# Clustered attention and a Hyena layer on one core: the written order of the steps drawn anew from group 6's scores on

## The chip, the cores and the metric

The kernel runs on one core of one Trainium2 chip. The time is the device time of one execution in microseconds (us); less is better. A core has the engines PE (matrix products), DVE, ACT and POOL (element work of several kinds), SP (which issues transfers) and 16 DMA engines. Each engine works through a queue of its own in order and waits at an instruction until what it needs is there.

## The reference, cut

```python
q, k, v: (4, 8, 768, 64); centroids: (8, 16, 64)
q_assign = argmax(einsum('bhsd,hcd->bhsc', q_n, c_n))      # q, k, centroids normed
k_assign = argmax(einsum('bhsd,hcd->bhsc', k_n, c_n))
scores = 1/sqrt(64) * q @ k.T, where(q_assign == k_assign), else -1e9
attn = softmax(scores);  x = (attn @ v) laid out as (4, 768, 512)

proj = x @ w_proj;  x1, x2, x3 = proj split in three      # w_proj (512, 1536)
x2_conv = irfft(rfft(x2) * rfft(filter))                  # along the 768 positions
out = (x1 * x2_conv * x3) @ w_out                         # (4, 768, 512)
```

## The kernel before, in words

**Tiling.** The 32 heads are worked in 8 groups of four heads (group 6 is the second last), each group in two halves of two heads. Two groups make one of the four batches, and behind every second group stands the Hyena layer of that batch.

**A half of a group** (`attention`): for each of six key tiles three score products into one PSUM bank each (L643, in 64-column halves by `product`, L71), three exps on ACT (L657, L660) into a `p` tile, one product with v (L671, "pv"), and on DVE the sum of the `p` tiles (L688 for the first two, L692 "acc" for the others). The row sums in `acc` are then folded by POOL's accumulating DMAs (L725), go through DRAM by SP (L729 dd, L731 dp), are summed on DVE (L735), inverted (L737), and come back spread over the partitions (L738 dr, L742 rb). L772 multiplies with them and writes `xT`, the input of the Hyena layer.

**The routing of the next group** (`routing`): loads of q and k (L286) into four `qkraw` buffers, a transpose on DVE, called the swap here (L560), copies to the `aug` tiles, products with the centroids (L589, "sim"), transposes (L594), the maximum (L602), the one-hot (L603), its transpose (L606), a prefix product on PE (L610, of the transposed one-hot), its two forms on ACT (L612, L617), and mask transfers of them into `aug` by SP (L491). The v loads are L301.

**The Hyena layer** (`hyena`): U products (L809) and their sums and differences, products with the DFT table and with the filter's spectrum (L833, whose results L837 adds), G products (L71 on behalf of L875) with the gate on DVE (L886) or a copy on ACT, the inverse transform I, the folds (L922), the product y2 (L929 in two parts for the last, L934), the output products W (L945 for earlier batches, L951 for the last, there in a first part of three quarters and a last quarter), copies out of PSUM (L957) and outputs (L966, in the last batch's end L962, from SP or ACT). In the last batch, negated tables (L846 and the two copies at L850 and L852) are written into load buffer `qkraw[0]`, so they need the swap that reads it last to be over.

**What sets the order.** No scheduler runs: the string `ORDER` (L126 to L229) lists all 1,976 steps of the program, each as a letter of an engine and the number of the step, and for a step that takes PSUM banks the banks behind a colon. `P1053:3` is step 1053 on PE into bank 3. Each engine's queue is this list cut down to its letter, and a step waits for the steps that it depends on and for the last reader of its bank. Steps that read or write SBUF heavily on DVE and POOL are marked as locked: a locked POOL step waits for the last locked DVE steps ahead of it in the list; a DVE step doesn't wait for a POOL step.

Of the kernel before, what the change touches and what calls it, by code (L numbers as in the profile page):

```python
# [126 lines left out]
A30 S43 P0:7 G12 A42 P1:6 S44 G23 P2:7 V16 A34 A48 P3:6 S41 G22 A46 P4:7 P5:6 S47 G17 G14 G11 P6:7 V49 P7:6 G19 S45  # L127
V31 P8:7 G29 V50 P9:6 P10:7 V32 V33 V51 A35 A36 V52 V15 P72:6 V37 G24 P70:7 A53 G18 A54 S126 V73 P38:5 A71 S125 V55
P66:4 V39 G20 P64:3 A67 V56 S124 A65 P78:4 V57 S123 A69 V58 P76:3 A62 V75 A60 V79 A59 G61 P101:7 G74 V77 A63 P99:6 G27
V80 P95:4 S130 P93:2 G13 V96 A102 S127 V21 A100 V81 P144:4 P151:3 A94 S128 P252:7 V82 G68 P254:6 S129 A253 P146:2 G25  # L130
V145 A255 S122 V40 P88:7 P83:1 V152 A89 G103 P107:6 V147 S290 V84 A90 A153 V85 A98 P248:2 V104 P246:5 V92 G97 P185:3
V87 S286 A247 P192:4 S137 P105:0 G134 A186 V86 V91 A249 S287 P210:5 A193 V106 P258:3 P260:2 V108 G199 A259 P264:4 A261
V109 P266:3 A265 P196:7 G28 S301 P187:2 V110 A267 P194:4 G139 S295 A188 P220:0 V257 P270:63 S296 A221 V111 G26 A195
A211 G200 S136 P204:0 V272 P202:4 A197 P140:5 V271 P212:2 A203 P189:1 P222:7 S289 G250 V273 A213 S132 A190 P112:2
P148:6 A141 V115 P218:3 G201 P117:1 A223 P206:4 S133 V119 P214:5 A205 P230:7 V116 S298 A207 G138 P228:0 V150 V274 S300
A215 A263 S293 P191:45 V209 A269 S131 P198 A120 A113 V149 S291 G256 V275 A118 S292 A114 P208 G135 A121 V217 A229 S299
A219 P302:2 P321:1 A231 P309:0 S297 P276:6 V225 P226:3 A310 P216 A303 S294 A277 P304:2 A227 S288 V316 P279:0 P319:7
A322 P224 V233 A305 A268 P306:2 P232 A307 V159 A278 V157 A281 P313:2 V155 A234 P235:6 V160 A280 P311:1 P308:45 A314
V158 S283 A236 V433 G262 S245 A312 P327:6 S282 A251 P339:2 V439 G318 P323:0 P337:1 S237 P315 A328 V436 S463 A320 G317
S284 A324 V430 P347:6 S468 P335:3 A338 P329:7 S464 P331:0 V326 A340 P325 S285 A336 S465 A330 P373:3 A332 P343:2 S460  # L140
V162 P371:1 P345:7 A374 S472 P333 V334 A344 S459 A346 S458 P378:2 A434 P369:7 V163 P388:3 S461 P341 A348 V342 S362
A372 S238 A379 P376:1 S462 A370 P442:06 V384 S469 A377 V350 A432 S473 P390:1 P349 A389 S467 A391 V444 A431 G435 P398:3
V443 P476:1 P394:7 A351 G161 V445 P352:2 A395 P380:6 A399 P406:0 G154 V446 P404:7 P375:45 A353 A381 S354 V447 A405
P386:6 G383 A407 V239 P396:2 V716 P474:7 S240 P402:3 A387 P410:0 P382 A397 V719 G385 S746 A403 S355 A411 P412:3 G363
V156 P451:2 A477 P448:6 S745 P414:0 G368 P392 V164 A475 S242 A449 V393 S241 A450 P400 S470 A438 A453 V401 P481:6 A452
P485:7 A413 P166:1 S454 P408 A415 S466 A486 V356 V409 S455 A167 P165:0 S357 A482 P483:7 P495:3 P416 A171 S456 V417
A484 A496 P491:6 P478:7 A169 P499:2 V172 P419:3 G437 A479 V170 A500 G441 P174:7 A420 V168 P493:1 A418 G364 P511:2 S421
P509:3 V488 P173:0 G365 A492 P480:45 V243 A494 V244 A510 S422 V175 P507:1 A177 G489 P487 S359 V722 A508 S471 A512 G490
S749 V178 P655:1 P517:2 A656 P501:3 S358 V176 P503:7 A502 P519:6 P653:1 V498 P497 A504 A718 P660:7 A721 P515:3 P505
A440 V423 V506 S424 A516 S457 P513 A518 S534 A520 S429 V514 A654 P674:2 P662:3 S748 P657:6 A675 P670:0 S747 P680:1  # L150
A663 P521 S751 V725 A658 A681 V522 P728:36 A523 A671 A661 V360 P524:1 V361 P142:7 A525 P664:0 V730 S425 G668 P180:2
A665 V729 P672:1 S526 A143 P659:45 V731 A181 S426 A673 V669 P762:7 P682:1 V732 P179:0 A683 S527 P690:6 P678:3 A183
P666 V733 G667 S757 A679 V184 A691 P686:3 G367 A763 V182 P694:2 G366 P696:6 P688:1 A695 V528 P760:0 V427 S529 P764:7
A697 P676 V677 A765 A717 P684 A689 V428 A687 V685 P698:1 A761 P769:3 P734:7 A720 P692 A699 V693 A770 P771:1 P700 A735
S530 A736 S531 A772 V701 P737:7 P781:3 S744 A702 P767:0 P779:1 P785:6 S752 A738 P797:2 P766:45 A768 S750 A782 G703
S759 A786 P795:0 S756 A798 V532 A780 V533 A739 S758 V774 A724 P535:3 V886 G775 P537:2 V536 S914 P793:1 G776 P777:7
S740 V538 P789:3 P540:6 A778 V539 A726 S755 P787:7 V784 P542:2 A788 S753 A541 P545:7 S741 A790 G704 V543 P803:6 S754
P547:3 A546 V792 A804 P773 S915 A723 A794 V548 S743 P805:6 A727 V544 P801:1 G551 S742 P582:7 V549 A796 S822 P783 A806
V889 G553 A888 V895 S919 P791 A887 G705 S715 V800 A583 S917 P825:6 A890 P840:0 P842:3 P799 A802 V892 A826 A841 P823:1
V808 A843 P898:27 A824 V550 P852:3 P832:1 G810 P848:0 A853 S706 V900 P844:6 S929 P807 A833 V899 G552 S923 A849 V901  # L160
P554:0 A809 S918 V902 P557:7 P830:2 A845 P834:1 P827:3 V555 A831 S916 P578:6 G838 V556 A828 P934:2 A579 V558 P829:45
S926 A835 G837 V559 S885 V903 P850:1 S707 P858:7 P860:6 S920 P864:0 A859 V839 P930:3 P836 A851 V561 G811 A861 S927
V847 A865 S921 P856:6 P562:1 A931 P866:0 A935 P565:7 V560 P963:3 A857 P868:2 P846 V855 A867 A893 P941:0 A869 P854 V564
A942 V863 A891 P932:0 P904:2 G812 P593:6 A933 A905 P907:0 V567 P862 A594 A906 V871 A909 P951:2 A908 P949:6 P870 A952
V563 A950 G569 V708 P570:2 A872 V566 S813 P937:1 G873 S924 P573:6 V709 A938 V568 S911 P965:0 P955:7 A966 V572 P939:1
S910 P936:45 A964 V1174 A956 G946 S814 A940 V1177 P957:3 P947:7 P973:0 P959:1 A948 S710 V571 P943 G944 A958 V575 A896
S928 V574 G945 P953 S1205 S925 G874 V954 A974 S922 A960 P1115:0 S712 P967:6 P975:1 A968 P1122:3 P1113:2 V576 P971:7
A976 P584:6 S1207 V962 A1123 P580:1 S913 A1114 P1132:3 A972 S711 P1118:2 P961 A1116 V577 S912 G875 A1119 V970 P1111:2
P586:70 A1112 P969 A587 V581 A894 V978 P1120:1 A897 P977 A1133 V589 P1130:2 G980 V588 P599:3 S876 A1131 V1180 P597:7
G590 A1121 V815 P1144:2 S1211 A598 P601:01 G591 V585 S1213 A1145 V1183 P1136:7 P595:6 A602 G592 A1137 V600 P1148:2  # L170
A1179 V816 P1186:73 V603 S817 A1149 V604 S877 A1175 V596 S1212 P1146:2 V713 P612:6 A1147 V606 P1220:1 V714 S1209 A613
P1140:0 P608:2 V1187 A979 G981 P1156:6 V1188 A1141 P1117:45 V1189 G1125 S819 A609 P1128:2 V1127 S1203 P1138:0 P1152:7
A1129 P1154:3 V1190 P1124 S818 A1139 A1157 S1206 V1126 A1153 S992 P1218:6 V605 P616:20 G982 A1221 V1135 A1219 P1222:7
P1229:1 P1134 A1155 A617 V878 A1223 G607 P1227:3 V1191 A1181 P1142 A1230 V879 V619 S880 A1228 P1192:1 V618 P1195:7
P1225:6 A1193 V1143 P1235:3 P614:2 A1184 S983 P1253:0 S1208 A1194 P1150 A1196 V820 A1197 V1151 A1226 P1158 S1198 A1236
S984 P627:6 V821 P610:3 V1234 S881 A1160 V621 P1237:7 S882 A628 P629:1 V615 A1185 V1159 P1239:2 P1263:6 A1238 P1224:45
A1240 V630 G620 P1247:2 P1251:1 A1248 P623:7 V985 G1161 A1252 V611 A624 V986 P631:32 V622 S987 A1264 S1199 P1245:1
A632 P1231 V883 A1246 V884 A1178 V633 P1255:6 G1232 P1243:1 V634 P625:7 A1244 V1347 P1259:3 A1254 G1233 P1261:2 P1241
S989 V626 A1348 S988 G1162 V1242 A1260 S1216 P1249 A1262 S1210 A1256 S1204 A1182 P1306:3 P1257 V1250 A1176 S1202 P1265
V990 S1200 V991 P1302:6 S1214 P1281:2 A1267 V1258 G1163 P1310:7 P993:0 S1215 A1282 P995:1 A994 S1217 V1266 A1311  # L180
P1003:2 S1378 A1303 P1290:7 P1005:6 A1004 V636 A1291 G1268 V996 P1308:2 P998:0 A1309 V1006 G635 A1307 V997 P1285:7
S1164 P1000:2 S1201 V1344 G637 A999 P1298:1 A1286 P1036:3 V1001 S1173 A1299 P1040:0 V1007 A1037 G1008 P1316:1 S1280
V1002 P1283:7 P1055:6 A1317 V1350 A1284 G1009 P1314:2 P1292:1 A1041 P1051:3 S1165 V1353 A1315 P1288:0 G1269 A1056
# [1052 lines left out]
```

## Time and profile before

| | |
|---|---|
| three timed runs, us | 351.40, 352.58, 352.62 (median 352.58) |
| the profiled execution's own time, us | 351.8 |
| its span, us | 350.0 |
| granted TensorE clock, mean | 0.997 |
| page's longest groups: pv products (L671), busy us on PE | 141.3 |
| exps L660 and L657, busy us on ACT | 108.8 and 56.3 |
| acc L692, busy us on DVE | 111.9 |
| DMA moved, MB | 45.68 |

Span and rows are those of one profiled execution; 1.8 us of its time lie outside the span. A row of the timeline gives the start, the length, the engine, the source line, the operation with its output and input, and how many instructions were put together; in brackets stands the idle time of the engine ahead of it and what ended that. In the page's groups, the busy time and the mean length of one stand behind the bar.

The end of the span is the output of the last batch: W products up to 344.5, copies, and transfers that move until 348.4.

### The profile page before, as it was taken

The numbers are of one execution on the slowest core, as the hardware profiler recorded it, in microseconds if no ns is written. First come the engines' busy times: TensorE is split into PE (matmuls) and PEld (weight loads), VectorE is DVE, ScalarE is ACT, GpSimd is POOL, SyncE is SP. The second block draws the span as 40 slices with busy tenths as digits, with TensorE's granted clock in tenths as the row PEclk, the third lists the DMA queues.
The fourth block names the chain that finished last, engine by engine and source line by source line (L and its number), as shares of the span: only waits on it lengthen the run. The fifth ranks groups of instructions, "written<-read, shape, count | busy, mean of one in ns | idle before, by whom it ended". The sixth has DMA issues, their size and how long they took to land.

```text
span 350.0 us, 8306 instructions
## 1 busy us (share of the span) xinstructions
PE 338.0 (97%) x3140; PEld 225.5 (64%) x3143; DVE 327.5 (94%) x453; ACT 274.4 (78%) x514; POOL 148.6 (42%) x175
## 2 busy tenths in 40 slices
PE   7899999999999999999999999999999999999993
PEld 3544455465756687866657687756677666678872
DVE  7999999999989999999999999989988999989992
ACT  5899999998989798889888798798896674433442
POOL 7486308232234517262337735461425034067610
PEclk9999999999999999999999999999999999999998
DMA  9989693997698997897697979655586411230044
GB/s 168 206 181 209 116 170 49 155 165 173 105 167 146 160 148 105 146 151 123 117 168 154 149 80 222 87 99 123 112 211 109 93 11 65 91 122 0 19 165 180
DMA packets 126323, 45.68 MB, mean 131 GB/s; under 512 B 113720, under 2 KB 118604, under 8 KB 126284
## 3 DMA queue, kind: packets, MB, share of 16 engines
q1 hardware_dynamic: 120396, 34.25, 50.4%
q0 software_dynamic: 2960, 9.77, 18.3%
q10 hardware_dynamic: 2928, 1.15, 1.4%
q8 instruction: 24, 0.39, 0.5%
q14 instruction: 15, 0.12, 0.2%
HBM read 31.59 MB, written 7.40 MB: 111 GB/s over the span
## 4 chain that ended last, share of the span: by engine, by line
PE 66%; ACT 15%; DMA 6%; DVE 4%; issue 4%; POOL 3%; SPq 1%; ACTq 0%; DVEq 0%; POOLq 0%
PE bank L71 32%; PE pair L671 24%; ACT p L660 6%; PE bank L809 5%; DMA qkraw<-in_q_dram 3%; ACT p L657 2%; ACT aug L249 2%; DMA dr<-dn 2%; PE bank L589 2%; ACT qkP L249 1%; DMA rb<-dr 1%; POOL acc L688 1%; DVE xT L772 1%; PE bank L478 1%; POOL uv L468 1%
## 5 line engine op out<-in xcount | busy, mean ns | idle before, releaser
L671 PE MATMUL pair<-p,vraw 128*64 128x385 f32 x768 | 141.3, 487 | 0.6 <-ACT p L660 0.6
L660 ACT ACTIVATE p<-bank 128x512 f32<-128x512 f32 x192 | 108.8, 605 | 12.1 <-PE bank L71 9.2
L692 DVE TENSOR_TENSOR acc<-p,acc 128x1536 f32<-128x1536 f32 x64 | 111.9, 1749 | 2.3 <-POOL acc L688 0.4
L671 PEld LDWEIGHTS pair<-p,vraw 128*64 128x64 f32 x768 | 66.8, 137 | 37.5 <-issue 22.2
L71 PE MATMUL bank<-aug 128*64 128x256 bf16 (+3 forms) x728 | 89.9, 329 | 1.0 <-ACT p L660 0.5
L71 PEld LDWEIGHTS <-aug 128*64 128x64 bf16 (+1 forms) x728 | 64.3, 153 | 29.2 <-issue 17.6
L657 ACT ACTIVATE p<-bank 128x512 f32<-128x512 f32 x96 | 56.3, 603 | 10.8 <-PE bank L71 10.1
L725 POOL DMA_DIRECT2D acc<-acc x30 | 24.0, 800 | 70.0 <-DMA acc<-acc 34.2
L688 POOL TENSOR_TENSOR acc<-p,p 128x512 f32<-128x512 f32 x32 | 40.7, 1302 | 25.8 <-DVE xT L772 13.6
L71 PE MATMUL bank<-xT,wpj 128*64 128x384 bf16 x512 | 50.8, 326 | 0.0
L249 ACT CAST aug<-qkP 64x768 bf16<-64x768 f32 x50 | 41.1, 830 | 1.0
L71 PEld LDWEIGHTS <-wpj 128*64 128x64 bf16 x512 | 35.6, 110 | 9.0 <-issue 2.3
L71 PEld LDWEIGHTS <-y 128*64 128x64 bf16 x472 | 27.0, 110 | 7.6 <-issue 1.5
L833 DVE TENSOR_TENSOR tm<-bank,hm 128x512 f32<-128x512 f32 x44 | 28.4, 679 | 1.2 <-ACT p L660 0.5
L922 POOL TENSOR_TENSOR yy<-sd 128x384 f32<-128x384 f32 x15 | 15.7, 1103 | 28.8 <-DVE y L934 14.4
L837 POOL TENSOR_TENSOR y<-tm 128x512 bf16<-128x512 f32 x13 | 16.5, 1274 | 22.9 <-DVE acc L692 11.1
L809 PE MATMUL bank<-wpj,xT 128*64 128x512 bf16 x192 | 23.7, 379 | 0.4 <-DVE xT L772 0.3
L560 DVE STREAM_TRANSPOSE qkP<-qkraw 128x768 f32<-128x768 f32 x24 | 22.3, 956 | 0.3 <-ACT aug L249 0.3
L71 PE MATMUL bank<-wout,y 128*64 128x512 bf16 (+1 forms) x192 | 22.2, 370 | 0.0
L249 ACT COPY ob<-bank 128x512 f32<-128x512 f32 x20 | 11.5, 588 | 12.5 <-PE bank L71 10.6
L251 POOL CAST aug<-qkP 64x768 bf16<-64x768 f32 x11 | 9.0, 819 | 26.7 <-DVE acc L692 9.4
L772 DVE SCALAR_TENSOR_TENSOR xT<-osb,rb 128x384 bf16<-128x384 f32 x30 | 17.7, 608 | 1.9 <-DMA rb<-dr 1.8
(155 smaller groups left out, 421.0 us busy)
## 6 DMA issues: line engine op xcount, KB each, us to landing
vraw<-in_v_dram SPq DMA_DIRECT2D x16, 384.0 KB, 5.2
rb<-dr SPq DMA_DIRECT2D x30, 192.0 KB, 3.4
qkraw<-in_k_dram SPq DMA_DIRECT2D x48, 96.0 KB, 4.5
qkraw<-in_q_dram SPq DMA_DIRECT2D x48, 96.0 KB, 4.7
out_dram<-ob SPq DMA_DIRECT2D x9, 512.0 KB, 3.0
acc<-acc POOLq DMA_DIRECT2D x10, 384.0 KB, 5.7
acc<-acc POOLq DMA_DIRECT2D x10, 192.0 KB, 4.3
wpj<-in_moe_w_proj_dram POOLq DMA_DIRECT2D x4, 384.0 KB, 4.7
```

The source lines that it names most:

```text
L71: T.nc.tensor.matmul(out[64 * i:64 * i + 64], lhsT[:, 64 * i:64 * i + 64], rhs, start=start, stop=stop)
L249: T.nc.scalar.copy(out, in_)
L560: op(("DVE", .9), lambda e, s=s, j=j, pr=pr: V().transpose(T.qkP[pr][:, S * j:S * j + S], T.qkraw[s][:].rearrange("p t h d -> p (t h d)")) ...
L657: T.nc.scalar.activation(o, ap(h).rearrange("p (a b) -> p a b", a=2), Act.Exp, scale=0.125)
L660: T.nc.scalar.activation(flat(s)[:, lo:lo + 512], ap(h), Act.Exp, scale=0.125)
L671: T.nc.tensor.matmul(o[64 * hp:64 * hp + 64, ch, :385], T.vraw[vs][:, hp, sk * D:(sk + 1) * D], T.p[slots[sk]][:, hp, 384 * ch:384 * ch + ...
L688: alu(e).tensor_tensor(o, x, y, op=Alu.add)
L692: T.nc.vector.tensor_tensor(T.acc[os], T.p[slots[sk]][:, :, :S], T.acc[os], op=Alu.add)
L725: op(("POOL", .8), lambda e, rows=rows: T.nc.gpsimd.dma_start(flat_()[:rows], flat_()[rows:2 * rows], accum_op=Alu.add), te, r=[], w=AK, b ...
L772: op(("DVE", .32 if last else .6), lambda e, a_=a_, r=r: T.nc.vector.scalar_tensor_tensor(T.xT[xs][:, kt].rearrange("p (r w c) -> p r w c" ...
L809: T.nc.tensor.matmul(ap(h)[64 * i:64 * i + 64], T.xT[xs][:, kt, tokens(m, i, w_)], T.wpj[:, kt, DM:2 * DM], start=kt == 0, stop=kt == ND - 1)
L833: op(("DVE", .68), lambda e, i=i, cs=cs, r=r, h=h: T.nc.vector.tensor_tensor(T.tm[r][:, cs], ap(h), hmrow(i, (0, 2, 2, 3)[2 * r + cs]), op ...
```

## The change

Only the string `ORDER` differs; what a step computes, and all other code, stay. Read engine by engine, the queues are the same up to the sim products of group 6 near 193.7 us of the profile before. From there on the order of the steps on all engines is drawn anew: 158 steps take other banks, and 38 change the engine. Of these, 13 go from DVE to POOL (the two-input steps L468, L688, L837, L922 and two y2 products of L934), 12 of the same kinds without L934 from POOL to DVE, 7 copies from ACT to DVE and 3 back, 2 from ACT to POOL and one from POOL to ACT. PE has the same matrix products, in another order.

The lines of the list that show the first difference on PE:

```diff
@@ ORDER, two of its lines @@
-V1357 S1379 V1017 S1376 P1326:3 G1295 P1318:6 V1016 P1300:1 A1327 S1385 P1392:7 P1324:0 A1301 V1359 P1322:3 S1377
...
+V1014 S1379 A1345 P1287:45 V1358 G1297 S1376 V1357 S1385 P1053:1 G1295 S1377 P1326:3 P1318:6 V1054 S1372 A1327 V1017
```

**Near 195 us, DVE.** The queue of DVE behind the two transposes of group 6's sim (L594); `x_136` is the gated product of the Hyena layer, `tm` its spectrum product.

```order
 L594 STREAM_TRANSPOSE sim<-bank_64 128x384
 L594 STREAM_TRANSPOSE sim<-bank_67 128x384
+L886 TENSOR_TENSOR x_136<-bank_64,x_136 128x2x192
 L833 TENSOR_TENSOR tm_132<-bank_65,h_142 128x512
 L833 TENSOR_TENSOR tm_131<-bank_65,hm 128x512
```

A gate (step 1054) stands ahead of two L833 products, and with it, on PE, its G product (step 1053) directly behind a pv product. A few steps on, a second gate and a swap stand ahead of acc's:

```order
 L606 STREAM_TRANSPOSE ohT<-oh 128x768
-L737 RECIPROCAL dn<-dn 128x12
-L692 TENSOR_TENSOR acc_113<-p_101,acc_113 128x1536
+L560 STREAM_TRANSPOSE qkP_108<-qkraw_86 128x768
+L737 RECIPROCAL dn<-dn 128x12
 L886 TENSOR_TENSOR x_135<-bank_66,x_135 128x2x192
-L692 TENSOR_TENSOR acc_113<-p_102,acc_113 128x1536
-L692 TENSOR_TENSOR acc_113<-p_98,acc_113 128x1536
-L560 STREAM_TRANSPOSE qkP_108<-qkraw_86 128x768
+L692 TENSOR_TENSOR acc_113<-p_101,acc_113 128x1536
```

The swap (step 1635) has moved ahead of the reciprocal, the gate and three acc's. The W product of step 643, which ran at 221.9 us of the profile before, stands on PE behind this gate's bank now.

**The same place, SP.** The queue of SP behind the dd transfer that ran at 201.6 us.

```order
 L286 DMA qkraw_85<-in_q_dram 32x24x32
 L729 DMA dd_123<-acc_114 16x1536
-L731 DMA dp<-dd_123 128x16x12
-L738 DMA dr_124<-dn 128x12
-L491 DMA aug_92<-sim 16x1536
-L286 DMA qkraw_87<-in_q_dram 32x24x32
-L491 DMA aug_93<-sim 16x1536
-L491 DMA aug_94<-sim 16x1536
```

```order
+L491 DMA aug_94<-sim 16x1536
+L491 DMA aug_93<-sim 16x1536
+L738 DMA dr_124<-dn 128x12
+L286 DMA qkraw_85<-in_q_dram 32x24x32
+L731 DMA dp<-dd_123 128x16x12
```

The second piece is what follows dd now: two mask transfers ahead of dr, a load and dp.

**The tables near 226 us, ACT.** Before, the row of L846 with its neighbours, and after it the same row in its new place.

```order
L660 ACTIVATE p_101<-bank_64 128x512
L846 ACTIVATE qkraw_85<-inv 128x768
L249 COPY ob_133<-bank_65 128x512
L249 COPY ob_133<-bank_67 128x512
L249 COPY qkraw_85<-inv 64x768
L660 ACTIVATE p_98<-bank_66 128x512
L249 COPY qkraw_85<-inv 64x384
```

```order
L249 CAST aug_93<-qkP_109 64x768
L657 ACTIVATE p_102<-bank_64 128x2x256
L846 ACTIVATE qkraw_85<-inv 128x768
L695 COPY osb_116<-pair_471 128x770
L660 ACTIVATE p_99<-bank_67 128x512
```

L846 is the 378th row of ACT's queue before and the 433rd now; the first copy is the 453rd, and the second goes to POOL.

**The end, PE's W products and ACT.** The W products of the last batch, by their steps in the order in which PE ends them: before 1949, 1957, 1973, 1953, 1961, 1969, 1965, with the parts of the last ones in between; now 1949, 1965, 1957, 1973, 1961, 1953, 1969. Ahead of 1949 stood five first parts, and now two. The last steps of DVE before the copies are two gates (L886), two folds (L922) and the two halves of the last y2 (L929). They stood as fold, fold, gate, gate, y2, y2, and stand now as gate, fold, y2, gate, fold, y2. ACT's last rows before and now:

```order
L249 COPY ob_134<-bank_66 128x512
L249 COPY tm_131<-bank_68 128x256
L962 DMA out_dram<-ob_134 128x512
L249 COPY ob_134<-bank_67 128x512
L962 DMA out_dram<-tm_131 128x256
L249 COPY tm_131<-bank_66 128x512
L962 DMA out_dram<-tm_131 128x256
```

```order
L249 COPY ob_133<-bank_65 128x512
L249 COPY tm_131<-bank_67 128x512
L249 COPY tm_131<-bank_66 128x256
L962 DMA out_dram<-ob_134 128x512
L249 COPY ob_133<-bank_67 128x512
L962 DMA out_dram<-tm_131 128x256 x2
```

The copy of the first W product is ACT's first row of the second list.

More of the change, by code (lines that the diff above doesn't have):

```diff
@@ L132 @@
[L132 to L136, printed above, removed]
@@ new lines @@
+P515:3 P505 V423 V506 S424 A440 S457 A516 P513 S534 A518 V514 A520 S429 A654 P674:2 S748 P662:3 P657:6 A675 P670:0
+S747 P680:1 A663 V725 P521 S751 A658 V522 A681 P728:36 A523 A671 V360 A661 P524:1 V361 P142:7 V730 A525 P664:0 S425
+G668 P180:2 V729 A665 S526 P672:1 A143 P659:45 V731 A181 S426 A673 V669 P762:7 V732 P682:1 P179:0 A683 P690:6 P678:3
+A183 V733 G667 S527 P666 S757 A679 V184 A691 G367 P686:3 V182 A763 P694:2 G366 P696:6 P688:1 A695 V528 P760:0 V427
+S529 P764:7 A697 P676 V677 A765 A717 P684 A689 V428 A687 V685 P698:1 A761 P769:3 P734:7 A720 P692 A699 V693 A770
```

192 lines of the change are left out of this document (96 added, 96 removed).

## The prediction, made before the run

> **What bounds the kernel now.** I read the page's busy line first, then the stretches, then the waits of single engines. The page is of one execution with a span of 350.0 us; the execution itself took 351.8, so 1.8 us lie around the span. The median of the three timed runs, 352.58, is 0.78 us above that execution.
>
> ```profile
> span 350.0 us, 8306 instructions
> PE 338.0 (97%) x3140; PEld 225.5 (64%) x3143; DVE 327.5 (94%) x453; ACT 274.4 (78%) x514; POOL 148.6 (42%) x175
> ```
>
> The stretches show where it is tight. The columns are the stretch, its length, busy time (instructions) of PE, PEld, DVE, ACT, POOL, then the granted TensorE clock, the DMA share and GB/s.
>
> ```profile
> 193.70:205.00 11.30, 11.22 (x97) 8.64 (x95) 11.26 (x15) 9.15 (x17) 5.22 (x5) 1.00 0.93 134
> 205.00:217.00 12.00, 12.00 (x114) 9.99 (x112) 11.40 (x16) 10.60 (x19) 7.84 (x7) 1.00 0.87 160
> 217.00:232.00 15.00, 14.51 (x150) 9.95 (x147) 13.86 (x19) 12.94 (x26) 6.63 (x7) 1.00 0.68 94
> 232.00:260.00 28.00, 28.00 (x267) 18.49 (x269) 26.93 (x33) 25.73 (x48) 8.29 (x8) 1.00 0.66 150
> 300.00:343.00 43.00, 42.95 (x536) 32.54 (x534) 39.03 (x69) 16.58 (x34) 19.21 (x16) 1.00 0.20 72
> 343.00:350.00 7.00, 1.56 (x20) 0.86 (x14) 1.16 (x3) 1.78 (x4) 0.00 (x0) 0.86 0.60 225
> ```
>
> PE is busy nearly without a gap at a clock of 1.00, and the two kernels give it the same matmuls. So the change can win only two things: PE gaps, and time after the last matmul. In the six rows the PE gaps sum to 0.08 + 0.49 + 0.05 up to 343; allowing for matmuls that overlapped less than usual, I count about 1.75 us of PE time over pure streaming after 193.7. **DVE is the second bound**: 11.26 of 11.30 us at the place where the change begins. Whatever makes PE wait for DVE there is not caught up soon.
>
> **Term 1, the stall that goes (-0.8).** Near 229 PE is held by exp work.
>
> ```profile
> 229.63 0.90 PE L71 MATMUL bank<-aug 80*64 80x256 bf16 x8 [0.49 <-ACT p L660]
> 226.56 0.85 ACT L846 ACTIVATE qkraw<-inv 128x768 bf16<-128x768 bf16 x1
> 227.29 1.08 ACT L249 COPY ob<-bank 128x512 f32<-128x512 f32 x2
> 228.24 0.84 ACT L249 COPY qkraw<-inv 64x768 bf16<-64x768 bf16 x1
> 228.97 0.60 ACT L660 ACTIVATE p<-bank 128x512 f32<-128x512 f32 x1
> ```
>
> The negated table of L846 is written over a load buffer, so it sits in ACT's queue until DVE's swap of L560 has read that buffer; then it and its continuation cost ACT 0.85 + 0.84 us ahead of the exp that frees PE's bank. In the changed order the tables stand some 50 rows further down in ACT's queue, the last of the three on POOL, and the swap stands earlier in DVE's. I take the 0.49 us idle and the 0.34 us by which the matmuls ahead of it ran slow: **-0.83**. About 0.2 us of other small waits in that stretch go too. The cover for the moved tables is ACT's idle time behind 260: 16.58 busy of 43.00 us after 300.
>
> **Term 2, a wait that comes (+1.3).** At 195 the order draws two hyena gate products forward: a G product that ran at 208.6 goes right behind the pv product, its gate (L886) goes ahead of two L833 products on DVE, and a W product (L945) goes from 221.9 to 202.8 with a bank that another gate frees. These are the rows of before (PE, then DVE).
>
> ```profile
> 195.02 1.81 PE L71 MATMUL bank<-aug 128*64 128x512 bf16 x16
> 200.69 0.90 PE L71 MATMUL bank<-xT,wpj 128*64 128x384 bf16 x8
> 193.87 1.05 DVE L594 STREAM_TRANSPOSE sim<-bank 128x384 f32<-128x384 f32 x2
> 194.84 0.65 DVE L833 TENSOR_TENSOR tm<-bank,h 128x512 f32<-128x512 f32 x1
> ...
> 196.01 0.93 DVE L602 TENSOR_REDUCE mx<-sim 128x48 f32<-128x768 f32 x1
> 196.95 1.76 DVE L692 TENSOR_TENSOR acc<-p,acc 128x1536 f32<-128x1536 f32 x1
> 198.62 0.95 DVE L603 TENSOR_TENSOR oh<-sim,mx 128x768 bf16<-128x768 f32 x1
> ...
> 199.91 0.98 DVE L606 STREAM_TRANSPOSE ohT<-oh 128x768 bf16<-128x768 bf16 x1
> 200.81 0.20 DVE L737 RECIPROCAL dn<-dn 128x12 f32<-128x12 f32 x1
> 202.54 0.55 DVE L886 TENSOR_TENSOR x<-bank,x 128x384 f32<-128x384 f32 x1
> 206.46 0.97 DVE L560 STREAM_TRANSPOSE qkP<-qkraw 128x768 f32<-128x768 f32 x1
> ```
>
> Step by step. The G product takes 0.90, so it runs 195.0 to 195.9. DVE has ended its transposes at 194.9 and **waits for it until 196.0: 1.1 us** in which the L833 products, the maximum, acc, the one-hot and its transpose all stand behind the gate. From 196.0 the same rows one after another come to about 6.4 us (0.55 gate, 0.65, 0.67, 0.93, 1.76, 0.95, 0.52, 0.98, less some 0.6 by which starts overlap the preceding ends in the rows): the one-hot's transpose ends at about 202.5 where it ended at 200.9. Behind it stands now a swap (0.97, moved up from 206.46), then 0.20 and the gate 0.55: the gate is through at 204.2. The W product wants its bank at 202.8 by PE's own streaming. It waits until about 204.3, **1.5 us, against 0.22 us of lag that PE had there before: +1.3**. I find no second binding wait for PE up to 260, since DVE's new order puts group 7's swaps ahead of acc's that stood in front of them, and with them what PE needs next. Bounds: 1.2 if the swap overlaps more, 1.9 if its load is late.
>
> **Term 3, nearer loads (0, bounded).** The queue of SP is reordered in the same place.
>
> ```profile
> 201.62 0.45 SPq L729 DMA_DIRECT2D dd<-acc  x1
> 204.50 0.38 SPq L731 DMA_DIRECT2D dp<-dd  x1
> 204.99 1.22 SPq L738 DMA_DIRECT2D dr<-dn  x1
> qkraw<-in_q_dram SPq DMA_DIRECT2D x48, 96.0 KB, 4.7
> ```
>
> Two of the mask transfers (L491) stand directly behind dd now. They need the one-hot's prefix results, which follow the W product of term 2, so SP stands still until about 206.5 (204.5 before), and dr, dp, the q and k loads and rb wait behind them. Loads that were issued 12 to 15 us ahead of their swap are issued 4.6 to 6 us ahead. With the page's median of 4.7 us to landing, the q load that the first of these swaps needs, issued near 209, lands at about 213.5, and the k load at about 215; DVE, by the sum of its rows in the new order, reaches their swaps at 215.5 and 216.4. It fits by 1 to 2 us, so I take 0. The bounds are -0.3 (SP is free sooner for the rest) and +2.5 (each transfer takes half as long again at the DMA share of 0.87 and the swaps stall DVE, of which PE feels all but some 1.5 us).
>
> **Term 4, engine changes (0).** 13 small DVE steps go to POOL and 12 come back; a few copies change between ACT and DVE. They are of the same kinds, so DVE's work stays the same within 1 us, and POOL has room (6.63 busy of 15.00, 19.21 of 43.00 in the stretches). The first row below is the kind of step that leads to the last I products: in the new order such a one ends on POOL near 330.0 again, by the sum of POOL's rows, and its partner on DVE near 330.5, and PE wants both at 331.2. So there are 0.7 us of cover, and PE is late once they are used up. Bounds: -0.3, and +1.3 (one such step more, behind the other).
>
> ```profile
> 328.86 1.27 POOL L837 TENSOR_TENSOR y<-tm 128x512 bf16<-128x512 f32 x1 [0.41 <-DVE tm L833]
> 54.61 1.23 DVE L603 TENSOR_TENSOR oh<-sim,mx 128x768 bf16<-128x768 f32 x1
> 53.74 1.28 POOL L468 TENSOR_TENSOR uv<-tm,tm 128x512 bf16<-128x512 f32 x1
> ```
>
> Beside a POOL step L603 took 1.23 us, alone (above, 198.62) 0.95, so a partly overlapped POOL step costs some 0.3 us here. The kernel lets a POOL step wait for the DVE step ahead of it in the order, which keeps most pairs apart, and the 13 steps that move are met by 12 that come back. (The Trainium skill, "SBUF — State Buffer", section "Who interferes with whom", states that a DVE instruction with two SBUF inputs and a GpSimd instruction that reads SBUF exclude each other for the whole instruction. That speaks against the 13 steps on POOL. By it the sum would be up to 1.3 us higher; the row above, 0.3 us longer with most of a 1.28 us step alongside, shows a wait for the part still to run, not the whole, since the POOL step began first.)
>
> **Term 5, the tail (-0.85).** The last part of the span is not PE but output.
>
> ```profile
> 342.54 1.29 DVE L251 COPY ob<-bank 128x512 f32<-128x512 f32 x2 [0.71 <-PE bank L71]
> 342.75 0.59 ACT L249 COPY ob<-bank 128x512 f32<-128x512 f32 x1 [4.13 <-PE bank L71]
> 343.26 1.73 SPq L962 DMA_DIRECT2D out_dram<-ob  x3
> 345.20 0.85 SPq L962 DMA_DIRECT2D out_dram<-tm  x1
> DMA packets 1008, 1.57 MB, mean 225 GB/s; under 512 B 112, under 2 KB 368, under 8 KB 1008
> DMA  0000006999999999999999999899994000000000
> GB/s 0 0 0 0 0 0 246 386 386 374 351 375 386 410 351 398 345 374 363 328 392 375 380 357 374 322 375 427 386 374 152 0 0 0 0 0 0 0 0 0
> ```
>
> The last two rows cut 343 to 350 into 40 slices of 0.175 us: six transfers' worth, 1.57 MB, move without a hole from 344.1 to 348.4 at about 370 GB/s. None is issued before 343.26, because the six last W products each get their last quarter only at the end. In the changed order the gate, the fold and the half of y2 that the first one needs (L929) come first on DVE, and its W stands behind two first parts in place of five: by PE's rows it ends at about 341.0, its copy at 341.6, so a first output of 262 KB leaves 1.65 us sooner. It is through before the rest, 1.31 MB, starts at about 344.05 (the copies of the others are where they were, 343.1 to 345.15). 1.31 MB at 370 GB/s is 3.54 us, so the output ends at 347.6 in place of 348.4: **-0.85**. It is -0.5 if the rest starts later, -1.0 if a second output gets ahead too, and 0 if the last copy decides.
>
> **Sum.** 350.0 + 1.3 - 0.83 - 0.2 - 0.85 = 349.4 us of span, 351.2 with the 1.8 us around it, and on the scale of the median (0.78 above the profiled execution) **352.0**: no change that can be told, since about 0.5% (1.76 us) is what a measurement of this kernel tells from none.
>
> **Rivals.**
> - *DVE starves for its loads at 203 to 217* (slower). Mechanism: SP stands behind the two mask transfers, the loads land over 6 us after issue in place of 4.7, and swaps at 202.5, 215.5 and 216.4 wait, DVE having only 0.04 us of slack in 11.3 there. It decides once the landings are over 2 us late: DVE loses 2 to 4 us, PE what lies beyond its 1.5 us; with term 2 at its 1.9 the sum is 352.0 + 0.6 + 1.0 to 3.0: **353.6 to 355.6**. For: the DMA share 0.93 and 0.87. Against: a DMA share under 0.7 from 217.
> - *POOL collides or is late* (slower, smaller): 0.5 to 1.3 us more, **352.5 to 353.3**, from the point where the 0.7 us of cover before 331 is used up.
> - *The tail does not shorten*: if the output is bound by its last issue, 345.2, the -0.85 falls away, **352.9**.
> - *Faster*: the DVE wait of 1.1 us is made good before PE reaches the W product (the swap ahead of it overlapped or its bank free earlier) and the tail gives 1.0: 352.0 - 1.2 - 0.2, **350.6** (350.2 to 351.0).
> - *The change moves nothing that binds*: the stall near 229 turns up a little later under another name. With term 1 gone this is 352.8.
>
> **How the numbers follow.** My forecast, with its own range 351.0 to 353.0, gets 0.48; the load rival 0.23; POOL 0.07; tail or stall unchanged, together 0.10; faster 0.12. The time predicted is the forecast's. The range for 8 in 10 reaches from the middle of the faster case, 350.4, to the lower half of the load rival, 354.4, and leaves some 0.05 below and 0.15 above. Faster by over 0.5% means under 350.8: most of the faster case, 0.10. Slower means over 354.3: two thirds of the load rival, 0.15, and 0.03 from POOL's outer bound together with a term 2 at its own. Within: 0.72.
>
> **What the changed profile would show.** Term 1: no table of L846 in front of an exp between 215 and 235, and no PE idle at 229. Term 2: DVE idle for about 1.1 us from 194.9, released by PE's bank, and PE idle 1 to 1.9 us near 203 ahead of a W product, released by DVE's gate. Term 3: swaps of L560 at 202 to 217 without an idle of DVE released by a DMA. Term 4: no PE wait for POOL at 331. Term 5: a first L962 issue near 341.6 and DMA busy that ends about 347.6 less whatever the body gains or loses. An idle DVE behind qkraw loads, or PE gaps of over 2 us in the 205 to 232 stretch, would make the forecast wrong on the slow side; a PE without any gap from 195 to 230 on the fast side.

## The result, and the profile after

The changed kernel took **355.37 us** (median of 22 runs, 352.63 to 359.78), the kernel before 352.83 (22 runs, 351.40 to 356.02). The ratio is **1.0054** with a 95% interval of 1.0029 to 1.0078: slower by about 1.9 us, 1.0 to 2.8. The medians lie further apart, by 2.5 us, because the ratio leaves out four slow runs of the changed kernel (358.7 to 359.8). The forecast was 352.0 with 350.4 to 354.4, so it missed on the slow side.

The profiled execution took 354.43 us, its span is 352.7. First the stretches of the profile after, with the columns of the prediction's table; then the waits of PE by what ended them: us in all, how many, the longest.

```profile
193.70:205.00 11.30, 10.92 (x99) 6.30 (x97) 9.57 (x15) 9.49 (x17) 8.00 (x8) 1.00 0.96 146
205.00:217.00 12.00, 11.21 (x96) 7.21 (x97) 11.97 (x16) 8.89 (x18) 5.04 (x6) 1.00 0.51 72
217.00:232.00 15.00, 14.26 (x131) 9.33 (x129) 12.63 (x14) 10.92 (x20) 5.81 (x7) 1.00 0.82 138
232.00:260.00 28.00, 28.00 (x285) 19.72 (x285) 27.53 (x41) 22.54 (x42) 11.17 (x10) 1.00 0.71 128
```

```profile
PE bank L71 <- DVE x L886: 1.2, 3, 0.6
PE bank L71 <- ACT p L660: 0.4, 1, 0.4
PE bank L71 <- ACT p L657: 0.2, 1, 0.2
```

DVE, which was busy 11.26 of 11.30 us in the first stretch, now idles 1.7 us there, and PE waits three times for a DVE gate. PE's idle up to 232 grew from 0.57 to 1.91 us, and behind 232 there is again none. DVE's timeline shows where its idle time is (in brackets, with what ended it).

```profile
197.59 0.56 DVE L886 TENSOR_TENSOR x<-bank,x 128x384 f32<-128x384 f32 x1 [0.83 <-PE bank L71]
...
203.08 0.97 DVE L606 STREAM_TRANSPOSE ohT<-oh 128x768 bf16<-128x768 bf16 x1
204.81 0.98 DVE L560 STREAM_TRANSPOSE qkP<-qkraw 128x768 f32<-128x768 f32 x1 [0.76 <-DMA qkraw<-in_k_dram]
205.71 0.19 DVE L737 RECIPROCAL dn<-dn 128x12 f32<-128x12 f32 x1
205.82 0.49 DVE L886 TENSOR_TENSOR x<-bank,x 128x384 f32<-128x384 f32 x1
...
217.86 0.97 DVE L560 STREAM_TRANSPOSE qkP<-qkraw 128x768 f32<-128x768 f32 x1
220.93 0.98 DVE L560 STREAM_TRANSPOSE qkP<-qkraw 128x768 f32<-128x768 f32 x1 [2.11 <-DMA qkraw<-in_k_dram]
```

Two of these three are **waits of a swap for its k load**, 0.76 and 2.11 us; the profile of before has no DVE wait on a load between 193 and 232. On PE the same places read as follows.

```profile
195.29 1.52 PE L671 MATMUL pair<-p,vraw 128*64 128x385 f32 x8
198.20 1.13 PE L71 MATMUL bank<-aug 80*64 80x256 bf16 x12 [0.31 <-DVE x L886]
205.44 0.35 PE L71 MATMUL bank<-ohT,tri 128*64 128x384 bf16 x2 [0.44 <-ACT p L660]
206.36 1.05 PE L71 MATMUL bank<-wout,y 128*64 128x512 bf16 x8 [0.35 <-DVE x L886]
231.50 0.68 PE L71 MATMUL bank<-aug 128*64 128x512 bf16 x4 [0.57 <-DVE x L886]
```

**How the profiles are compared.** The pv product that began at 193.67 in before begins at 195.29 here, although every queue is the same up to that place. In the 15 profiles of this study whose queues are the same up to there, before's among them, that entry lies between 193.35 and 196.66 us. So I measure from the entry on, in two ways: **entry to end** (156.31 us in before, 157.41 here) and **PE's lag** (a step's start, less the entry, less the sum of the usual lengths of PE's steps between; the more waits, the larger it is). The lag at the end of the matmuls is 1.75 us in before and 3.77 here. It is 1.94 at the W product near 206 and 3.01 at the next sim products, near 236; at the W product it is reached by +0.48 and +0.29 (early gate), +0.63 (the prefix product, behind an exp on ACT) and +0.54 (the gate behind the swap).

The end of the profile after, the outputs' DMA in slices of 0.2425 us from 343:

```profile
344.48 0.59 ACT L249 COPY ob<-bank 128x512 f32<-128x512 f32 x1 [2.41 <-PE bank L71]
345.10 0.34 SPq L962 DMA_DIRECT2D out_dram<-ob  x1
DMA  0000000000008980005999999999999991000000
```

One output leaves at 345.1, 3.1 us before the last matmul ends (348.19), and is through before the others start. From the last matmul to the end of the span it is 4.50 us, where before took 5.43: **the end gives 0.93 us**.

### The profile page after: what moved, and what is told of

Read it like the earlier page. It is cut to its first block, busy times and chain, and to the rows that moved or that the text cites. A ratio compares the mean times of both kernels' runs of the same rounds, so it can differ in the third digit from the quotient of the medians.

```text
span 352.7 us, 8317 instructions
## 1 busy us (share of the span) xinstructions
PE 337.8 (96%) x3141; PEld 218.3 (62%) x3143; DVE 328.5 (93%) x456; ACT 272.5 (77%) x509; POOL 152.2 (43%) x177
## 4 chain that ended last, share of the span: by engine, by line
PE 53%; DVE 16%; DMA 8%; issue 4%; ACT 3%; SPq 2%; POOL 1%; DVEq 0%; ACTq 0%
PE bank L71 29%; PE pair L671 18%; DVE acc L692 7%; PE bank L809 3%; DVE qkP L560 2%; DMA dr<-dn 2%; DMA acc<-acc 1%; DMA qkraw<-in_k_dram 1%; DMA qkraw<-in_q_dram 1%; POOL acc L688 1%; ACT p L660 1%; DMA rb<-dr 1%; PE bank L589 1%; SPq L286 1%; DVE tm L821 1%
## 5 line engine op out<-in xcount | busy, mean ns | idle before, releaser
L71 PE MATMUL bank<-aug 80*64 80x512 bf16 (+3 forms) x728 | 88.2, 329 | 2.6 <-DVE x L886 0.9
L671 PEld LDWEIGHTS pair<-p,vraw 128*64 128x64 f32 x768 | 64.4, 137 | 39.1 <-issue 25.9
L688 POOL TENSOR_TENSOR acc<-p,p 128x512 f32<-128x512 f32 x32 | 40.6, 1283 | 35.5 <-ACT p L660 13.6
L71 PE MATMUL bank<-xT,wpj 128*64 128x384 bf16 x504 | 49.6, 326 | 0.2 <-ACT p L657 0.2
L71 PEld LDWEIGHTS <-wpj 128*64 128x64 bf16 x504 | 33.0, 110 | 12.8 <-issue 4.2
L71 PEld LDWEIGHTS <-y 128*64 128x64 bf16 x480 | 25.9, 110 | 10.4 <-issue 2.2
L833 DVE TENSOR_TENSOR tm<-bank,hm 128x512 f32<-128x512 f32 x44 | 28.4, 680 | 0.7 <-POOL y L837 0.2
L934 POOL TENSOR_TENSOR y<-yy,x 128x768 bf16<-128x768 f32 x10 | 18.3, 1829 | 20.1 <-PE bank L71 12.5
L71 PE MATMUL bank<-wout,y 128*64 128x512 bf16 (+1 forms) x200 | 23.2, 371 | 0.4 <-DVE x L886 0.3
L837 POOL TENSOR_TENSOR y<-tm 128x512 bf16<-128x512 f32 x15 | 19.3, 1306 | 8.1 <-DVE acc L692 7.1
L249 ACT COPY ob<-bank 128x512 f32<-128x512 f32 x18 | 10.5, 589 | 15.6 <-PE bank L71 12.1
L922 POOL TENSOR_TENSOR yy<-sd 128x384 f32<-128x384 f32 x12 | 12.9, 1106 | 18.6 <-DVE acc L692 12.4
```

The source lines that it names most:

```text
L71: T.nc.tensor.matmul(out[64 * i:64 * i + 64], lhsT[:, 64 * i:64 * i + 64], rhs, start=start, stop=stop)
L249: T.nc.scalar.copy(out, in_)
L671: T.nc.tensor.matmul(o[64 * hp:64 * hp + 64, ch, :385], T.vraw[vs][:, hp, sk * D:(sk + 1) * D], T.p[slots[sk]][:, hp, 384 * ch:384 * ch + ...
L688: alu(e).tensor_tensor(o, x, y, op=Alu.add)
L833: op(("DVE", .68), lambda e, i=i, cs=cs, r=r, h=h: T.nc.vector.tensor_tensor(T.tm[r][:, cs], ap(h), hmrow(i, (0, 2, 2, 3)[2 * r + cs]), op ...
L837: op({"POOL": 1.3, "DVE": .68}, lambda e, i=i, r=r: alu(e).tensor_tensor(T.y[:, i, r], T.tm[r][:, 0], T.tm[r][:, 1], op=Alu.add if r else ...
```

## The experiments

Theory A: loads of group 7's q and k now land so near their swaps that DVE, which has no slack, waits for them, and PE with it. Rivals: the early gates, ACT's order, or the engine changes and the middle of the order cost by themselves. The edits move words of `ORDER` alone (a shared piece keeps its banks, save where a seam, the place at which two orders are joined, needs another free one). All ratios are to before, with the 95% interval; the changed kernel has 1.0054 (1.0029 to 1.0078). The four batches ran one after the other.

### Which part of the order

**tail_after**: before up to the last inverse product, then the changed order.

```diff
+ORDER = before[:1935] + (words of the change that are left, in its order)
```

> The order of before up to the last inverse product (near 333 us), and from there the changed order. Theory A (the changed end is worth about 1 us, and all of the loss lies ahead of it): the outputs' DMA ends about 1.1 us earlier after the last matmul than in before, median 0.8 to 1.1 us under before. Rival (the gap in the changed profile between last matmul and end is by chance, or the changed end is bound by its last copy): within 0.3 us of before.

Ratio 0.9997 (0.9972 to 1.0022), median 352.97. The time from the last matmul to the end fell to 4.01 us, but PE lost 0.96 us more than before from the entry to the last matmul, most of it behind the seam, where banks had to be taken anew. Entry to end is 155.84, 0.5 us less than before. The time can't tell that from nothing. All kernels below that have the changed order from 193 us on to the end have 4.48 to 4.50 us there, and those that join it at 230 have 4.74 or 4.75, against 5.43 and 5.44 where the end is before's: the gain at the end is no accident.

**first_after** and **first_before**: the changed order up to about 230 us and then before's, and the reverse.

```diff
+first_after:  ORDER = after[:1374] + (the rest in before's order)
+first_before: ORDER = before[:1375] + (the rest in the changed order)
```

> The changed order up to about 230 us, and from there the order of before, its end included. Theory A (the loss is in 195 to 230: early gates and loads that land too near their swaps): PE loses 1.5 to 2 us more than before between the first pv product behind group 6's sim and 232 us; median 1.0 to 2.0 us over before (no gain at the end here). Rival (the engine changes and the middle part lose): within 0.4 us of before.

> The order of before up to about 230 us, and from there the changed order, its end included. Theory A: the stall of 0.8 us near 229 stays as in before, the middle costs up to 0.3 us, the end gives 1.0: median 0.5 to 1.0 us under before. Rival (the loss lies in the engine changes behind 232): 0.3 to 1.3 us over before.

first_after has 1.0145 (1.0106 to 1.0184), median 357.50; first_before 0.9977 (0.9954 to 1.0001), median 351.97. In first_after the lag was 3.95 us by 228.7, more than was expected, and DVE waited for dp 0.87, for q 1.30, for k 0.91 and 0.43, and for rb 1.35 us. A further 3.3 us came at the seam (a wait of 2.84 us for a fold on POOL), so the size is not the change's. Still, the two together say it: **the loss is in the first 35 us**; the changed order behind 230, with its end and most of its engine changes, loses nothing that the time can tell.

### The loads

**loads_first**: five loads ahead of the mask transfers.

```diff
-S1271 ... S1370 S1369 S1168 S1373 S1272 S1375 S1368 S1374 S1384 S1386
+S1271 S1373 S1375 S1374 S1384 S1386 ... S1370 S1369 S1168 S1272 S1368
```

> The changed order, with five loads of group 7's q and k (L286) moved on SP from behind the two mask transfers to right behind the dd transfer at 204, so that they go out in the 4 us in which SP stands still. Theory A (loads behind the masks land too late): DVE's 2.1 us wait for the k load near 219 goes, and the wait of PE for a gate near 231 shrinks by 0.5 to 0.9 us; median 0.5 to 1.0 us under the changed kernel, that is 1.0 to 1.5 us over before. Rival (the DMA engines are full in this stretch, so earlier issues only queue): no less wait, same time as the changed kernel, about 1.9 us over before.

Ratio 1.0019 (0.9989 to 1.0049), median 353.38. The wait near 219 is gone, and there is no PE wait at the gate near 231. The other load wait, at 204, was 1.75 us in this run.

**swap_later** moves the swap near 204 behind two acc's; **gate_later** takes the early gate back.

```diff
-swap_later: ... V1635 P1042:3 A1319 V1167 A1398 V1043 ... V1058 A1366 V1321
+swap_later: ... P1042:3 A1319 V1167 A1398 V1043 ... V1058 A1366 V1321 V1635
-gate_later: P1053:1 ... V1054 ... P1057:1 ... V1058
+gate_later: P1053:1 ... V1054 (where P1057 and V1058 stood) ... P1057 V1058 (some 35 words further down)
```

> The changed order with one word moved: the swap (L560) that stood ahead of the gate near 204 goes behind the next two acc's on DVE. Theory B (the swap is drawn ahead of a gate for which PE waits, and its k load lands only then): DVE's idle of 0.8 to 1.8 us on that load goes, the lag of PE at the W product near 206 falls from 1.9 to about 1.4 us (what the prefix product leaves); the wait near 219 for another load stays; median 0.4 to 1.2 us under the changed kernel, 0.7 to 1.5 over before. Rival (DVE has no slack, so the order on it only moves the wait): same lag at 232, same time as the changed kernel.

> The changed order with the early G product (step 1053, near 195) and its gate put where the next G product and gate stood, and that next one a little further down. Theory C (the gate ahead of DVE's queue costs by itself): DVE's idle of 0.8 to 1.1 us at 195 goes, PE's lag at the first W product falls from 0.8 to 0.1 us and stays that much lower at 232; median 0.6 to 0.9 us under the changed kernel. Rival (the k load lands at a fixed time, so what DVE wins at 195 it waits for at 204): lag at the W product near 206 as before the edit, 1.9 us or less by at most 0.2; median within 0.3 us of the changed kernel.

swap_later: 1.0026 (1.0003 to 1.0049), median 353.81; lag 1.40 at the W product, as expected, and the later swap waited 1.52 us for its k load. gate_later: **1.0127** (1.0091 to 1.0163), median 357.11 of 6 runs. DVE's idle at 195 went, but the swap then waited 1.47 us for its load, and the new place of the second gate made waits of its own (DVE idle 1.68 and 0.95 us behind PE near 215). So this edit does not price the gate; what it shows is that the time won ahead of the swap did not arrive.

**exp_earlier** does the same on ACT.

```diff
-A1354 V1166 G1346 A1389 ... A1393 ... A1400 V1635 P1042:3 A1319
+A1354 A1319 V1166 G1346 A1389 ... A1393 ... A1400 V1635 P1042:3
```

> The changed order with one word moved: the exp that frees the bank of the prefix product (L610) near 204 goes ahead of three other steps on ACT. Theory D (ACT's order is a loss by itself): PE's lag at the prefix product falls from 1.4 to 0.8 us, and at the W product behind it to 1.5 or less; median 0.3 to 0.7 us under the changed kernel. Rival (the W product waits for the gate behind the swap and its load anyhow): lag at the W product 1.9 us or more, median within 0.3 us of the changed kernel.

Ratio 1.0100 (1.0061 to 1.0140), median 356.15 of 6 runs: the rival. The wait of the prefix product went, and PE's next wait took it all, and more (lag 3.05 at the W product). PE's row in this run:

```profile
206.59 1.05 PE L71 MATMUL bank<-wout,y 128*64 128x512 bf16 x8 [1.76 <-DVE x L886]
```

and DVE's, the load again:

```profile
205.03 0.98 DVE L560 STREAM_TRANSPOSE qkP<-qkraw 128x768 f32<-128x768 f32 x1 [1.86 <-DMA qkraw<-in_k_dram]
```

**three_undone** joins loads_first, swap_later and exp_earlier; **gate_too** adds the gate.

> The changed order with three edits: five loads ahead of the mask transfers on SP, the swap behind two acc's, and the exp of the prefix product's bank ahead of two other steps on ACT. Theory A with B (the load waits and ACT's order are the loss, the early gate a part of it): lag of PE at 232 between 0.7 and 1.0 us in place of 3.0, no DVE idle on a load between 195 and 232, median 0.3 to 0.9 us under before. Rival (scatter of landings decides anew, other loads are late): lag over 1.5, median over before by 0.3 or more.

> The three edits and the gate put later as well. Theory A with B and C: lag of PE at 232 between 0.1 and 0.5 us, no DVE idle over 0.3 us in 195 to 232, the end of the changed order kept; entry to end 1.5 us shorter than in before, median 1.0 to 1.6 us under before. Rival (the gate's place is not a cost by itself): the same time as with three edits, within 0.3 us.

three_undone: 1.0002 (0.9976 to 1.0029), median 353.08; no DVE wait on a load, but PE's lag at its sim products was 1.89, not under 1.0, which is the rival's; the time is level with before, not 0.3 to 0.9 us under it as expected, though its interval reaches there. gate_too: 1.0005 (0.9975 to 1.0036), median 353.35; the gate gave nothing beyond, as its rival had it. In its profile an acc met a POOL step (last section) and took 1.07 us more.

**after_again** is the changed kernel once more; **sp_alone** is before with only SP's order changed.

```diff
-sp_alone: S1271 S1272 S1168 S1368 S1380 S1369 S1370 S1375 S1170 S1169 S1373 S1374 S642 S1371 S1384 S1386 S1381 S1382
+sp_alone: S1271 S1370 S1369 S1168 S1373 S1272 S1375 S1368 S1374 S1384 S1386 S1169 S1371 S1382 S1170 S1381 S1380 S642
```

> The changed kernel once more, for a second profile beside the other edits. Theory A (the loss is waits on loads whose landing scatters): DVE again idles on qkraw loads between 200 and 222, by other amounts than the 0.8 and 2.1 us of the first profile; PE's lag at 232 between 2 and 4 us; median 1.0 to 2.8 us over before. Rival (the first profile's waits were an accident of that run): no idle of DVE on a load, lag under 1.5.

> The order of before, with only SP's 18 transfers between the dd transfer at 201.6 and 222 us in their changed order (two mask transfers ahead of dr, the loads and dp). Theory A (what costs is the distance from landing to use, and in before the swaps come at 225): no DVE idle on a qkraw load, PE's lag at 232 within 0.3 us of before, median within 0.7 us of before. Rival (SP standing behind the masks costs by itself, through dr, dp and rb): DVE waits for dp or rb, median 0.7 us or more over before.

after_again: 1.0049 (1.0024 to 1.0075), median 354.42; DVE waited 0.87 us for k at 206, 0.90 for dp at 217, 1.13 for q at 221; lag 3.14 at the sim products. Other sizes, the same places. sp_alone: 0.9996 (0.9968 to 1.0024), lag 1.00 at its sim products (1.22 in before). **SP's new order costs nothing that can be told where the swaps come late.**

### What sets the loss

In six profiles the swap near 204 stands ahead of the gate, waits for its load, and PE waits for that gate. In five of them the lag at the W product is the swap's start less the entry less 7.58 us, to 0.01, and the swap starts 0.12 or 0.13 us after the last of its k loads has landed:

| profile | last k load issued, us | landed, us | swap starts, us | entry, us | difference of the last two less 7.58 | lag measured |
|---|---|---|---|---|---|---|
| after | 199.54 | 204.69 | 204.81 | 195.29 | 1.94 | 1.94 |
| after_again | 200.96 | 206.03 | 206.16 | 196.53 | 2.05 | 2.05 |
| first_after | 198.34 | 203.42 | 203.54 | 193.88 | 2.08 | 2.09 |
| loads_first | 198.83 | 203.93 | 204.05 | 193.54 | 2.93 | 2.94 |
| exp_earlier | 199.34 | 204.91 | 205.03 | 194.41 | 3.04 | 3.05 |

(gate_later moves one G product of 0.65 us behind the W product. Its sum gives 1.84; PE's steps ahead of the W product are 0.65 us shorter there, so the lag is 2.49.) In all six DVE is idle until the load lands. The issue of that load began 4.2 to 5.3 us behind the entry, and it landed 5.1 to 5.6 us after its issue began. What PE or DVE did before that does not matter, which is why two edits that take waits away there could not pay. In the profile after, SP issued the loads behind two others that stood still until 193 for a buffer, although their own was free from 176.5. So the last question was put to SP alone.

**k_first** moves three k loads ahead of those two; **k_and_loads** adds the five of loads_first; **all_early** adds gate_later and exp_earlier.

```diff
-S1165 ... S1387 ... S1383 ... S1343 ... S1379 ... S1376 ... S1385 ... S1377
+S1165 S1376 S1377 S1379 ... S1387 ... S1383 ... S1343 ... S1385
```

> The changed order with only three k loads on SP (of the swap near 204) moved ahead of two loads for which SP waits at 193. Theory (their landing sets the swap, and the swap the gate for which PE waits): no DVE idle on a load near 204; PE's lag at the W product near 206 1.2 to 1.5 us in every run in place of 1.9 to 3.0; the waits on loads at 217 to 222 stay; median 0.5 to 1.3 us under the changed kernel. Rival (DMA engines are full there, the landing comes no earlier, or the two loads that are pushed back are late in their place): lag 1.9 or more, same time as the changed kernel.

> k_first with the five loads of loads_first as well; PE, DVE, ACT and POOL keep the changed order, only SP's differs. Theory (the loss is loads too near their swaps, all of it): no DVE idle on a load in 195 to 232, PE's lag at 232 1.3 to 1.7 us against 3.0, median between 0.6 us under and 0.4 us over before. Rival (the engines' order loses too): over before by 0.8 us or more.

> k_and_loads with the later gate of gate_later and the earlier exp of exp_earlier, each of which made the changed kernel no faster by itself. Theory (they were swallowed by the wait for the load): now they pay, PE's lag at 232 0.3 to 1.0 us, median 0.5 to 1.5 us under k_and_loads. Rival (they cost by themselves): the same time as k_and_loads or more.

k_first: 1.0022 (0.9998 to 1.0046), median 353.46; no wait at 204, lag 1.40 at the W product, and the later load waits stay (1.14 for dp, 1.37 for q, 0.41 for k; lag 3.43 at sim). k_and_loads: **1.0001** (0.9973 to 1.0029), median 352.51. DVE's waits between 193 and 233 in its profile are one row:

```profile
DVE x L886 <- PE bank L71: 0.9, 1, 0.9
```

and the swaps follow the steps ahead of them with no gap:

```profile
202.59 0.97 DVE L606 STREAM_TRANSPOSE ohT<-oh 128x768 bf16<-128x768 bf16 x1
203.48 0.94 DVE L560 STREAM_TRANSPOSE qkP<-qkraw 128x768 f32<-128x768 f32 x1
...
214.48 2.48 DVE L833 TENSOR_TENSOR tm<-bank,hm 128x512 f32<-128x512 f32 x4
216.87 1.83 DVE L560 STREAM_TRANSPOSE qkP<-qkraw 128x768 f32<-128x768 f32 x2
```

PE's lag is 1.40 at the W product and 1.28 at the sim products, and PE has no wait between. With PE's, DVE's, ACT's and POOL's queues exactly as changed, eight loads on SP take the whole loss away (the intervals of the two kernels just touch, at 1.0029). Entry to end is 155.65 us, 0.7 under before, which the time can't tell from nothing. all_early: 1.0002 (0.9975 to 1.0029), median 353.38. Its lag at the W product is 1.16 in place of 1.40, with the moved G product left out of the sum, but the later gate gives 0.47 back at that product and the lag at the sim products is 1.53: the rival, no gain.

### A version that might beat both

**best** is first_before with two moves at the seam, and **best_again** the same kernel once more.

```diff
-... P645:0 A644 ... A646 G1438 V1273 A1589 ... P1586:1 A1634 A1587
+... P645:0 A644 ... G1438 V1273 A1589 A646 ... P1586:1 A1587 A1634
```

> The order of before up to about 230 us, then the changed order with its end, and two moves on ACT at the seam (an output copy behind an exp, an exp ahead of a cast), each for a PE wait of 0.3 us seen in the run with the first part of before. Theory (with no nearer loads, the removed stall and the end are left as gains): PE's lag at 235 about 0.5 us in place of 1.3, median 1.0 to 1.8 us under before. Rival (the seam's waits move on): within 0.3 us of that run, 0.8 us under before.

> The version named best once more: the order of before up to about 230 us, then the changed order, with two moves on ACT. Expected as its last profile showed, PE's lag at 235 0.5 us, entry to end 1.0 us under before, median 0.5 to 1.3 us under before. Rival: within 0.3 us of before.

best: 0.9987 (0.9955 to 1.0019), median 351.50, lag 0.49 at the sim products as expected, entry to end 155.34. best_again: 1.0005 (0.9973 to 1.0036), median 354.05, lag 1.00, entry to end 155.6. The profiles show 0.7 to 1.0 us less from the entry on; the runs, with their scatter of 4 us, don't confirm it. No version was shown to beat before.

## Why the prediction was wrong, point by point

**The miss is term 3, and the load in term 2.** "It fits by 1 to 2 us, so I take 0" was the step that failed: the k load of the second swap was to land at about 215, ahead of the swap's turn at 216.4, and the swap waited 2.11 us for it. Step by step against k_and_loads, whose PE, DVE, ACT and POOL queues are the same, PE lost 0.36 us near 224 and 0.78 near 231 behind these later transfers. In after_again the waits were 0.90 for dp and 1.13 for q, and PE lost 0.60 and 0.57. With the 0.53 (0.65) at the W product this makes 1.7 (1.9) us at the sim products, where term 3 had 0.

Where the sum went wrong is seen in the rows of SP in the profile after.

```profile
208.63 1.15 SPq L491 DMA_DIRECT2D aug<-sim  x2
209.88 0.52 SPq L738 DMA_DIRECT2D dr<-dn  x1
210.44 1.06 SPq L286 DMA_DIRECT2D qkraw<-in_q_dram  x1
211.61 0.47 SPq L731 DMA_DIRECT2D dp<-dd  x1
212.12 1.56 SPq L286 DMA_DIRECT2D qkraw<-in_q_dram  x1
213.73 0.53 SPq L491 DMA_DIRECT2D aug<-sim  x1
214.30 0.58 SPq L286 DMA_DIRECT2D qkraw<-in_q_dram  x1
214.93 1.14 SPq L286 DMA_DIRECT2D qkraw<-in_k_dram  x2
```

A landing at 215 with 4.7 us puts the last k load's issue near 210.3; it began at 215.55. Of these 5.2 us the entry of this profile, 1.6 us later than before's, explains a part, and SP starts on the masks another 0.5 us late. The largest part, 3.1 us, is SP's own work: from the first mask to this load it takes 6.9 us where I had allowed 3.8. From the start of the issue to the swap's start it is 5.4 us against 4.7. So **the issue time was the larger error and the time to landing the smaller**: I had counted one median from issue times on SP that I had only worked out.

For the swap near 202.5 I did not even put that median beside the issue. The last of its loads is issued between 199.07 and 200.87 in before's trace, and 4.7 us from there is 203.8 at the earliest, 1.3 us after the swap's turn. I weighed the distance only for the later swaps. "Bounds: 1.2 if the swap overlaps more, 1.9 if its load is late" had as its outer end what was the middle: over the five profiles of the table the lag was 1.9 to 3.0, which is 1.7 to 2.8 over before's 0.22.

**The load rival named the right wait**, with its price of 353.6 to 355.6 against 355.37 measured and a chance of 0.23. It should have been the likeliest. The price is 1.6 to 3.6 us over the forecast; the loads were worth 1.9 by the ratios of the changed kernel and k_and_loads, so that the median lies near the upper end owes something to luck. Its mechanism was right only in part. The loads of the later swaps did stand behind the masks and came late, but by late issue, not by landing "over 6 us after issue": where a swap waited and the landing is recorded, the load landed 5.1 to 5.9 us after its issue began. The load of the first swap stood behind the two loads that waited for a buffer, not behind the masks. And its point of decision, "over 2 us late", was too far: DVE had no slack, so any lateness counted.

**The other terms held, as far as one profile tells.** k_and_loads is the changed kernel with the loads in time, the case that I had summed. My sum was -0.6 us (350.0 to 349.4) and that profile has -0.7 from entry to end.
- Term 1: no L846 in ACT's rows ahead of an exp near 229, and in k_and_loads PE has no wait between 206 and 246. Right.
- Term 2 without the load: lag 1.40 against 0.22 of before, +1.2 for +1.3. DVE's idle for the early gate was 0.83 to 1.04 us for 1.1. One part I had not seen: 0.63 us of it came from ACT, where the exp of the prefix product's bank stands behind casts now, and not from DVE.
- Term 4: no PE wait for POOL near 331. Right, as far as the profiles go.
- Term 5: 0.93 us for 0.85. Right.

**On the shared port**, I read "a wait for the part still to run, not the whole" out of a row "with most of a 1.28 us step alongside". That reading of the row was wrong: the POOL step began at 53.74 and ended at 55.02, so only 0.41 us of it ran beside L603, which began at 54.61 and took 0.28 us longer. The Trainium skill ("SBUF — State Buffer", section "Who interferes with whom") calls the contention on this port an exclusive lock; that whoever issues first has it for the whole instruction and the other fully blocks, it states for DVE's 2-port modes. The row in the last section agrees with such a lock: the second loses nearly all that is left of the first. My reading and the rule come to the same where POOL began first.

**Open:** why exp_earlier and gate_later came out slower than the changed kernel (1.0100 and 1.0127 against 1.0049 and 1.0054) and not just as slow. Their profiles are slower too, with lags of 4.20 and 4.55 at the sim products against 3.01 and 3.14. In exp_earlier the load near 204 was issued 0.5 to 0.7 us later from the entry than in the two profiles of the changed kernel and took 0.4 to 0.5 us longer to land; why, the table doesn't say, and six runs each don't settle it. Nor does the lag of one profile give the order of the medians: k_first had 3.43 at the sim products with 1.0022, and the changed kernel 3.01 with 1.0054. That the medians lose by the loads rests on k_and_loads, not on the lags.

## What to carry to other kernels

Where a step waits for a load, write the issue time of that load plus the measured time to landing beside the step's turn, for every such step that a new order moves up. Take the issue time from the transfers that stand ahead in the queue, each with the time that it took in the trace, and take the scatter of issue and landing as the range, not a median. An engine that is busy 11.26 of 11.30 us turns each late load into lost time, and whatever is improved ahead of the wait is swallowed by it. Such a loss can be mended in the queue of the transfers alone: here eight loads, put ahead of others that stood still for a buffer or a mask, were worth the whole 0.5%.

## What the runs showed of the hardware that was not expected

- The same program up to the same place is there between 193.35 and 196.66 us from the span's start, in 15 profiles; a single profile of this kernel can't be compared by its span to better than some 3 us.
- One and the same load, behind the same queue up to the entry, was issued 4.2 to 5.3 us behind that entry and landed 5.1 to 5.6 us after its issue began (five profiles of the table). Its issue alone took 1.1 to 1.9 us of SP's time.
- In gate_too an acc that began 0.3 us behind a POOL step took 2.82 us, where the same acc took 1.75 in the other profiles; POOL's step ended at 201.72, 1.19 us after the acc's start, and 1.07 us is what the acc lost. It is one such pair, and the profile's spans on POOL are rough.

```profile
200.22 1.50 POOL L837 TENSOR_TENSOR y<-tm 128x512 bf16<-128x512 f32 x1
200.53 2.82 DVE L692 TENSOR_TENSOR acc<-p,acc 128x1536 f32<-128x1536 f32 x1 [0.36 <-POOL acc L688]
```
